# The first expert layer in scaled fp16 hi/lo pairs instead of f32r pairs, with whole-matrix staging

## The chip, the core and the metric

One core of one Trainium2 chip runs the whole program. The metric is the device time of one execution in microseconds (us); lower is better. TensorE (PE) does the matrix products, and loads the stationary operand of each (PEld). VectorE (DVE), ScalarE (ACT) and GpSimd (POOL) do the elementwise work. SyncE (SP) issues most of the transfers. Each engine runs its own instructions in their order and waits on semaphores of the others.

## The reference

Attention with a learned position bias comes first, then a dense mixture of four experts, then a routed one of eight.

```python
scores = q @ k.T / 8 + bias(i, j)            # batch 2, 8 heads, 576 tokens, 64 wide
x = softmax(scores) @ v                       # -> x: 1152 tokens x 512
p = domain_probs / (domain_probs.sum(-1) + 1e-9)
out = 0
for e in range(4):                            # _moe_ref, "the first expert layer"
    h = maximum(x @ w1[e], 0)                 # w1[e]: 512 x 1024
    out += p[:, e] * (h @ w2[e])              # w2[e]: 1024 x 512
# _moe2_ref: each token goes to the one of 8 experts (argmax of x @ w_gate),
# out = gate * sigmoid(x @ w_output_gate)[e] * (relu(x @ w1[e]) @ w2[e])
```

All inputs and the output are fp32, and the products must be close to fp32 ones. So each operand is held as a rounded part (hi) and a remainder (lo), and one product is three matmuls: hi·hi, hi·lo and lo·hi.

## The kernel before

The program has three stages. **Attention** works through 72 heads: index n runs from -2 to 77, u = n // 8 is a block of 128 query rows and h = n % 8 the head. One pass of the loop works on several heads at once: `soft_max(n+2)` on DVE, `soft_exp(n+1)` on ACT, `e_trans(n)` on PE, `qk(n+3)` on PE, `split_lo(n-1)` on DVE and `av(n-2)` on PE. `qk` needs `qt`, the transposed queries of four heads, whose halves two DMAs swap between partitions (L154, L155). The position bias of a block pair goes from `bo` by DMA into the tile `bias` (L311). The last block (u = 8) holds the ends of both batches, so its bias tile (`bias4`) takes two such DMAs for each piece; they are issued in passes n = 45 to 51. The attention weights `eth`/`etl` and v are already fp16 pairs.

**The first expert layer** is one loop over 96 passes i = 8·m + f, where m = 3·e + c is an expert and a chunk of 384 tokens and f a block of 128 hidden columns. Pass i does `l1(i)`, 12 matmuls of 384 columns, and `l2(i-2)`, 9 matmuls of 512 columns; the last eight blocks of l2 run as `l2_tile`. Between them ACT writes the hi part and DVE the lo part of h.

**The second expert layer** runs 13 slots of 128 gathered tokens. While its slot 0 runs, DVE and PE make a table of slots (`slot_table`, three steps), and SP reads its result to choose the expert whose weights it loads.

Every operand of the first expert layer is an f32r pair, 4 bytes an element. A weight matrix is four pieces of 512 KB. Each piece is loaded into a small staging tile (`st`, two of them, L438), and split into two big tiles by ACT and DVE (L457, L458) or, for six pieces that fall into the attention stage (the table `W0`), by POOL alone (L454, L455). The next load is issued when a piece is split. The order of instructions on each engine is the order of the code; the compiler moves a few matmuls of the first l1 ahead of the last attention work. The eight big tiles (`bigt`) are handed out as earlier ones are released. The attention's v is divided by a power of two found on chip (`vP`, its reciprocal `vR`), and `av_norm` (L405) multiplies that back.

Of the kernel before, what the change touches and what calls it, by code (L numbers as in the profile page):

```python
# [24 lines left out]
FF = 1024  # L25
# [25 lines left out]
W0 = {54: (1, 0), 57: (1, 1), 64: (1, 2), 66: (1, 3), 69: (2, 0), 71: (2, 1)}  # L51
# [4 lines left out]
def attn_moe_moe_kernel(ctx, tc, q, k, v, w1, b1, w2, dp, mw1, mw2, wg, wog, ew1, ew2, cst, lmc, out):  # L56
# [5 lines left out]
    st_p = ctx.enter_context(tc.tile_pool(name="st", bufs=2))  # L62
    attn = ExitStack()
# [335 lines left out]
    def av_norm(g):  # L399
        u = g // 2  # L400
        po = av_t.pop(g)
        if g % 2 == 0:
# [10 lines left out]
    xth = xtl = None  # L413
# [21 lines left out]
    def stage():
        e, w, k = pieces[len(staged)]
        t = st_p.tile([128, FF], F32, tag="st", name="st")
        sp.dma_start(out=t.rearrange("p (a d) -> p a d", a=2) if w == 2 else t, in_=msrc[w][e, k])  # L438
        staged[e, w, k] = t

    def pair(e, w, kinds):
        ts = [bigt(f"w{w}{e}", F32R, None) if p is big else p.tile([128, 4 * FF], F32R, tag="wx", name=f"w{w}{e}") for p in kinds]
        wt[e, w] = [[t[:, k * FF:k * FF + FF] for k in range(4)] for t in ts]

    def half(e, w):
        t = bigt(f"w{w}{e}", F32R, None)
        for i, l in enumerate(wt.setdefault((e, w), [[], []])):
            l += [t[:, k * FF:k * FF + FF] for k in (2 * i, 2 * i + 1)]

    def wsplit(e, w, k, on_pool=False):  # L450
        hi, lo = (l[k] for l in wt[e, w])
        t = staged[e, w, k]
        if on_pool:
            pool.tensor_tensor(out=hi, in0=t, in1=one.to_broadcast([128, FF]), op=ALU.mult)  # L454
            pool.tensor_tensor(out=lo, in0=t, in1=hi.bitcast(F32), op=ALU.subtract)  # L455
        else:
            act.copy(hi, t)  # L457
            dve.tensor_tensor(out=lo, in0=t, in1=hi.bitcast(F32), op=ALU.subtract)  # L458
        staged[e, w, k] = None
        if len(staged) < len(pieces):  # L460
            stage()

    with tc.manual_schedule():
# [76 lines left out]
        for n in range(-2, NT + 6):  # L540
# [698 lines left out]
```

## Time and profile before

| what | value |
|---|---|
| median of 3 runs | 855.02 us (850.95 to 857.32) |
| the profiled execution | 852.49 us |
| its span, first to last instruction | 850.6 us |
| busy PE / PEld / DVE / ACT / POOL | 793.2 / 671.2 / 490.7 / 392.8 / 181.6 us |
| mean granted TensorE clock | 0.987 |
| attention | 0 to about 251.7 us of the span |
| first expert layer | about 251.7 to 670 us |
| second expert layer | about 670 us to the end |

Busy time says which engine works, not which one sets the end: matmuls overlap in the records, and a matmul's time is best read from the distance between two starts. The granted clock is 1.00 at 2.4 GHz and 0.50 at 1.2 GHz. What ends an idle stretch stands in brackets behind a row of the timeline. The profiled execution lies 2.5 us below the median and 1.9 us above its own span; the sums below are made against its 852.49 us.

### The profile page before, as it was taken

The page shows a single profiled execution, that of the slowest core. Times are in us where ns is not written, and L with a number is a line of the kernel's source. Part 1 is how long each engine was busy: PE and PEld are TensorE (multiplying, and loading weights), DVE is VectorE, ACT ScalarE, POOL GpSimd, SP SyncE. Part 2 cuts the span into 40 slices and gives each one's busy share as a digit, 9 for nine tenths or more (in the row PEclk, how much of TensorE's full clock was granted, in tenths as well). Part 3 has the DMA queues.
Part 4 walks back from the last instruction along what each step waited for, and adds up shares of the span by engine and source line. Part 5 has one row for each costly group of instructions (what it writes and reads, how often), then busy time and mean ns, then how long its engine had stood idle before and what let it go on. Part 6 is the DMA issues. An engine that isn't in the chain of part 4 may idle for free.

```text
span 850.6 us, 14183 instructions
## 1 busy us (share of the span) xinstructions
PE 793.2 (93%) x5449; PEld 671.2 (79%) x5449; DVE 490.7 (58%) x880; ACT 392.8 (46%) x639; POOL 181.6 (21%) x157
## 2 busy tenths in 40 slices
PE   1877999997989999999999999999999879999996
PEld 0345778776879999999999999999997668888885
DVE  4989999995773312342214322142146859989993
ACT  1657899995643111231113211121123448888883
POOL 6737556651740000000000000000002022211110
PEclk9999999999999999999999999999999989999998
DMA  9944445579423100140002300010037639857720
GB/s 210 167 60 81 94 96 105 105 116 154 126 75 99 51 5 1 47 128 25 1 0 86 113 1 1 1 49 1 1 118 250 212 102 392 292 217 245 254 75 18
DMA packets 56984, 88.75 MB, mean 104 GB/s; under 512 B 18188, under 2 KB 26636, under 8 KB 56910
## 3 DMA queue, kind: packets, MB, share of 16 engines
q1 hardware_dynamic: 53152, 81.61, 36.0%
q0 software_dynamic: 2160, 6.06, 2.1%
q8 instruction: 45, 0.74, 0.4%
q10 hardware_dynamic: 1598, 0.11, 0.1%
q14 instruction: 29, 0.24, 0.1%
HBM read 82.75 MB, written 5.79 MB: 104 GB/s over the span
## 4 chain that ended last, share of the span: by engine, by line
PE 62%; issue 5%; DVE 3%; DMA 3%; ACT 1%; POOL 0%; POOLq 0%; DVEq 0%; ACTq 0%
PE hps L672 8%; PE hps L673 8%; PE hps L674 8%; PE yps L694 7%; PE yps L693 7%; PE yps L692 7%; PE l L994 5%; PE l L1023 5%; DMA out_x<-o,gs 2%; PE sc L324 1%; PE hp L1010 1%; DVE e L950 1%; PE lgp L779 1%; DMA raw<-in_moe_w 1%; PE etp L350 1%
## 5 line engine op out<-in xcount | busy, mean ns | idle before, releaser
L680 DVE SCALAR_TENSOR_TENSOR h<-hps,h 128x384 fp32r<-128x384 f32 x94 | 52.4, 557 | 256.5 <-ACT h L679 256.4
L679 ACT ACTIVATE h<-hps 128x384 fp32r<-128x384 f32 x94 | 46.2, 491 | 298.3 <-PE hps L674 298.3
L672 PE MATMUL hps<-xth,w 128*128 128x384 f32 x384 | 130.1, 339 | 0.0
L673 PE MATMUL hps<-xtl,w 128*128 128x384 f32 x384 | 129.6, 337 | 0.0
L674 PE MATMUL hps<-xth,w 128*128 128x384 f32 x384 | 129.2, 337 | 0.0
L950 DVE TENSOR_TENSOR e<-raw,e 128x1024 fp32r<-128x1024 f32 x104 | 121.1, 1220 | 7.8 <-ACT e L949 6.2
L694 PE MATMUL yps<-w,h 128*128 128x512 f32 x264 | 104.3, 395 | 0.0
L693 PE MATMUL yps<-w,h 128*128 128x512 f32 x264 | 104.0, 394 | 0.0
L692 PE MATMUL yps<-w,h 128*128 128x512 f32 x264 | 103.8, 393 | 0.0
L949 ACT CAST e<-raw 128x1024 fp32r<-128x1024 f32 x104 | 102.0, 1065 | 0.0
L966 POOL DMA_INDIRECT xg<-ydr,ids_e x3 | 5.1, 1691 | 396.0 <-DMA ydr<-y 395.4
L285 DVE TENSOR_SCALAR r<-lm,s,nb 128x576 f32<-128x576 f32 x89 | 75.6, 896 | 0.0
L673 PEld LDWEIGHTS hps<-xtl,w 128*128 128x128 f32 x384 | 72.2, 188 | 3.7
L672 PEld LDWEIGHTS hps<-xth,w 128*128 128x128 f32 x384 | 72.1, 188 | 3.7
L324 PE MATMUL sc<-kt,qt 128*128 128x288 f32 x320 | 61.8, 318 | 12.3 <-DVE mn L333 6.3
L674 PEld LDWEIGHTS hps<-xth,w 128*128 128x128 f32 x384 | 72.1, 188 | 0.0
L333 DVE CUSTOM_DVE_ANT_0 ns<-sc,bias 128x576 f32<-128x576 f32 x72 | 54.3, 754 | 23.0 <-PE sc L324 12.6
L324 PEld LDWEIGHTS sc<-kt,qt 128*128 128x128 f32 x320 | 45.9, 192 | 17.6 <-DVE mn L333 11.0
L694 PEld LDWEIGHTS yps<-w,h 128*128 128x128 f32 x264 | 49.6, 188 | 11.5
L343 ACT ACTIVATE e<-ns,mn 128x576 f32<-128x576 f32 x72 | 56.4, 783 | 0.0
L693 PEld LDWEIGHTS yps<-w,h 128*128 128x128 f32 x264 | 49.6, 188 | 8.0
L692 PEld LDWEIGHTS yps<-w,h 128*128 128x128 f32 x264 | 49.6, 188 | 7.6
(245 smaller groups left out, 1468.6 us busy)
## 6 DMA issues: line engine op xcount, KB each, us to landing
raw<-in_moe_w SPq DMA_DIRECT2D x104, 512.0 KB
st<-in_moe_w SPq DMA_DIRECT2D x32, 512.0 KB
bias<-bo SPq DMA_DIRECT2D x40, 288.0 KB
qt<-qt SPq DMA_DIRECT2D x40, 128.0 KB
ydr<-y SPq DMA_DIRECT2D x8, 258.0 KB
q<-in_q SPq DMA_DIRECT2D x8, 256.0 KB
kraw<-in_k SPq DMA_DIRECT2D x4, 512.0 KB
vraw<-in_v SPq DMA_DIRECT2D x8, 256.0 KB
```

What stands on the lines that cost most here:

```text
L285: (dve if on == "v" else pool).tensor_scalar(out=r, in0=src, scalar1=sc, scalar2=nb1, op0=ALU.mult, op1=ALU.max)
L324: pe.matmul(pt[:, z, 0:288], lhsT=t[w][:, h % 4, :], rhs=kk[:, h, z * 288:z * 288 + 288], start=(i == 0), stop=(i == len(seq) - 1))
L333: dve.tensor_tensor_reduce(out=ns.rearrange("p (z j) -> p z j", z=2), in0=pt[:, :, 0:288], in1=bias_t[u // 2][:, h, :].rearrange("p (z j) ...
L343: act.activation(out=e_t[n // 2][:, (h % 2) * S:(h % 2) * S + S], in_=ns, func=AF.Exp, scale=-1.0, bias=mn)
L672: pe.matmul(ps, lhsT=wh[k][:, fs], rhs=xth[:, c, k, :], start=(k == 0), stop=False)
L673: pe.matmul(ps, lhsT=wh[k][:, fs], rhs=xtl[:, c, k, :], start=False, stop=False)
L674: pe.matmul(ps, lhsT=wl[k][:, fs], rhs=xth[:, c, k, :], start=False, stop=(k == 3))
L692: pe.matmul(acc[m][t], lhsT=hh, rhs=wh[f // 2][:, ws], start=(f == 0), stop=False)
L693: pe.matmul(acc[m][t], lhsT=hh, rhs=wl[f // 2][:, ws], start=False, stop=False)
L694: pe.matmul(acc[m][t], lhsT=hl, rhs=wh[f // 2][:, ws], start=False, stop=(f == 7))
L949: act.copy(hi[:, k, :], raw[w][:, k, :])
L950: dve.tensor_tensor(out=lo[:, k, :], in0=raw[w][:, k, :], in1=hi[:, k, :].bitcast(F32), op=ALU.subtract)
```

## The change

It holds x, h and the weights of the first expert layer as fp16 pairs. fp16 has a small range of exponents, so each operand is scaled. x is multiplied by 8 in `av_norm`, and keeps v's power of two, which is put into the gate weights `pr` later. For each weight matrix the largest magnitude is found: four DVE reductions (`w_max`), one more over these, then a bounce through DRAM (`w_scale`: 128 maxima are written out, and read back into every partition as a row of 128), and a short DVE chain that makes the power of two P and the factor R. The scales go back out through `pr`, with the constant `YS`. The weights are loaded as a whole matrix into one big tile (`w_load`), since a matrix can't be split before its scale is known, and are split into one fp16 tile that holds hi and lo. ACT now writes every hi part with the scale; the lo part is one DVE instruction, or two on POOL for the four pieces of the first matrix. The table `plan` says in which pass a matrix is loaded, reduced and split. The second step of `slot_table` moves from the end of slot 0's first layer to behind the first six matmuls of slot 1's. [...]

```diff
-W0 = {54: (1, 0), 57: (1, 1), 64: (1, 2), 66: (1, 3), 69: (2, 0), 71: (2, 1)}
+W0 = {59: 0, 62: 1, 65: 2, 68: 3}
+XS = 8.0
+WS = {1: 2.0, 2: 16384.0}
+YS = 1.0 / (XS * WS[1] * WS[2])
...
+    def w_load(e, w):
+        t = wraw[e, w] = bigt("wraw", F32, None)[:, :4 * FF].rearrange("p (k f) -> p k f", k=4)
+        for k in range(4):
+            sp.dma_start(out=t[:, k].rearrange("p (a d) -> p a d", a=2) if w == 2 else t[:, k], in_=msrc[w][e, k])
+    def w_max(e, w, k):
+        dve.tensor_reduce(out=wm[:, k:k + 1], in_=wraw[e, w][:, k], axis=AX.X, op=ALU.max, apply_absolute_value=True)
+    def w_scale(e, w, q):
+        c = 2 * e + w - 1
+        dve.tensor_reduce(out=wm[:, 4:5], in_=wm[:, 0:4], axis=AX.X, op=ALU.max)
+        scr = ws_p.tile([128, 1], F32, name=f"scr{c}")
+        q.dma_start(out=scr, in_=wm[:, 4:5])
+        q.dma_start(out=wmb, in_=bass.AP(scr.tensor, scr.offset, [[0, 128], [1, 128]]))
+        yield
+        P, R = wP[:, c:c + 1], wR[:, c:c + 1]
+        dve.tensor_reduce(out=P, in_=wmb, axis=AX.X, op=ALU.max)
...
+    def w_split(e, w, k, on_pool=False):
+        hi, lo = wt[e, w][:, k, 0], wt[e, w][:, k, 1]
+        t, R = wraw[e, w][:, k], wR[:, 2 * e + w - 1:2 * e + w]
+        act.activation(out=hi, in_=t, func=AF.Copy, scale=R)
         if on_pool:
...
+            dve.scalar_tensor_tensor(out=lo, in0=t, scalar=R, in1=hi, op0=ALU.mult, op1=ALU.subtract)
...
+            if n == 44:
+                w_load(0, 1)
+            if 53 <= n < 57:
+                w_max(0, 1, n - 53)
+            if n == 57:
+                ws = w_scale(0, 1, pool)
+                next(ws)
+                w_tile(0, 1)
+            if n == 58:
+                next(ws)
             if n in W0:
-                wsplit(0, *W0[n], on_pool=True)
+                w_split(0, 1, W0[n], on_pool=True)
+            if n == 64:
+                w_load(0, 2)
+            if 70 <= n < 74:
+                w_max(0, 2, n - 70)
+            if n == 74:
+                ws = w_scale(0, 2, pool)
+                next(ws)
...
-            pe.matmul(ps, lhsT=wh[k][:, fs], rhs=xth[:, c, k, :], start=(k == 0), stop=False)
+            pe.matmul(ps, lhsT=w[:, k, 0, fs], rhs=xt[:, c, 0, k, :], start=(k == 0), stop=False)
...
+        plan = {(0, 2): (None, None, 0), (1, 1): (0, 4, 12), (1, 2): (5, 14, 20), (2, 1): (17, 26, 32), (2, 2): (25, 37, 43),
+                (3, 1): (37, 49, 56), (3, 2): (48, 60, 67)}
...
-        side = [[last, steps[2], steps[2], steps[2]], [(0, 0), last, lambda: x_in(1)], [(0, 1), tabs, last, last, (0, 2)], [(0, 3), tabs]]
+        side = [[last, steps[2], steps[2], steps[2]], [(0, 0), last, lambda: x_in(1)], [(0, 1), tabs, last, last, (0, 2)], [(0, 3)]]
...
-        side = [[], [lambda: h_in(0)], [last, lambda: ids_in(3)], [tabs]]
+        side = [[tabs], [lambda: h_in(0)], [last, lambda: ids_in(3)], [tabs]]
```

**SP's order in attention passes 42 to 47.** Before, the last DMA of `bias3` is followed by those of `bias4`, and then by the two qt swaps of pass 46 (a number behind a name tells tiles apart; the brackets hold what the instruction waits for, DMAHW being the lane that the transfer takes):

```order
L155 DMA qt_2569<-qt_2569 64x512 [waits DMAHW7_49]
L311 DMA bias3_1928<-bo_2604 16x8x576 [waits DMAHW0_49,Activation_49]
L311 DMA bias4_2695<-bo_2696 16x8x576 [waits DMAHW1_49,DVE_49,Activation_49]
L311 DMA bias4_2695<-bo_2696 16x8x576 [waits DMAHW2_49]
L154 DMA qt_2764<-qt_2764 64x512 [waits DMAHW3_49,Activation_49]
L155 DMA qt_2764<-qt_2764 64x512 [waits DMAHW4_49]
```

The same stretch now:

```order
L163 DMA qt_2574<-qt_2574 64x512 [waits DMAHW7_49]
L319 DMA bias3_1933<-bo_2609 16x8x576 [waits DMAHW0_49,Activation_49]
L446 DMA wraw_2700<-in_moe_w1 128x1024 [waits DMAHW1_49,DVE_49]
L446 DMA wraw_2700<-in_moe_w1 128x1024 [waits DMAHW2_49]
L446 DMA wraw_2700<-in_moe_w1 128x1024 [waits DMAHW3_49]
L446 DMA wraw_2700<-in_moe_w1 128x1024 [waits DMAHW4_49]
L319 DMA bias4_2705<-bo_2706 16x8x576 [waits DMAHW5_49,DVE_49,Activation_49]
L319 DMA bias4_2705<-bo_2706 16x8x576 [waits DMAHW6_49]
L162 DMA qt_2774<-qt_2774 64x512 [waits DMAHW7_49,Activation_49]
L163 DMA qt_2774<-qt_2774 64x512 [waits DMAHW0_49]
```

Four loads of 512 KB each now stand ahead of the bias transfers and of the qt swaps on the same queue.

**DVE's order in attention passes 57 to 59.** Before, from the end of pass 57:

```order
L362 SCALAR_TENSOR_TENSOR etl_3252<-etp_3206,eth_3215 128x512 [waits Activation_49]
L333 ISA ns_3302,mn_3303<-sc_3270,bias3_1928 128x576 [waits PE_49,Activation_49]
L333 ISA mn_3303 128x1
L405 TENSOR_SCALAR rc_3305<-avp_3154,vR_108 128x4 [waits PE_49]
L408 RECIPROCAL rc_3305<-rc_3305 128x4 [waits DVE_49]
L410 TENSOR_TENSOR x_3139<-avp_3154,rc_3305 128x256 [waits DVE_49]
L362 SCALAR_TENSOR_TENSOR etl_3312<-etp_3238,eth_3250 128x512 [waits Activation_49]
L333 ISA ns_3343,mn_3344<-sc_3314,bias3_1928 128x576 [waits PE_49,Activation_49]
```

Now, from the reduction that starts the bounce of the first matrix:

```order
L453 TENSOR_REDUCE wm_112<-wm_112 128x1 [waits DVE_49]
L341 ISA ns_3308,mn_3309<-sc_3275,bias3_1933 128x576 [waits PE_49,Activation_49]
L341 ISA mn_3309 128x1
L413 TENSOR_SCALAR rc_3311<-avp_3161 128x4 [waits PE_49]
L416 RECIPROCAL rc_3311<-rc_3311 128x4 [waits DVE_49]
L418 TENSOR_TENSOR x_3146<-avp_3161,rc_3311 128x256 [waits DVE_49]
L370 SCALAR_TENSOR_TENSOR etl_3318<-etp_3243,eth_3255 128x512 [waits Activation_49]
L459 TENSOR_REDUCE wP_110<-wmb_113 128x1 [waits DMASW1_49]
L460 TENSOR_SCALAR wP_110<-wP_110 128x1 [waits DVE_49]
L461 TENSOR_SCALAR wP_110<-wP_110 128x1 [waits DVE_49]
L462 RECIPROCAL wR_111<-wP_110 128x1 [waits DVE_49]
L341 ISA ns_3354,mn_3355<-sc_3320,bias3_1933 128x576 [waits PE_49,Activation_49]
```

(A fifth small instruction of the chain, L463, stands ahead of the last row.) One pass of work lies between the reduction L453 and L459, which waits for both DMAs of the bounce on POOL's queue and is ahead of the next `soft_max` (L341).

**DVE's order where the first expert layer begins.** Before, behind the last `av_norm` and the last x:

```order
L405 TENSOR_SCALAR rc_3990<-avp_3857,vR_108 128x4 [waits PE_49]
L408 RECIPROCAL rc_3990<-rc_3990 128x4 [waits DVE_49]
L410 TENSOR_TENSOR x_3847<-avp_3857,rc_3990 128x256 [waits DVE_49]
L429 TENSOR_TENSOR xtl_1079<-xtp_3994,xth_1078 128x4x128 [waits Activation_49]
L680 SCALAR_TENSOR_TENSOR h_4075<-hps_4062,h_4075 128x384 [waits Activation_49,Pool_49]
L458 TENSOR_TENSOR w20_4059<-st_3840,w20_4059 128x1024 [waits DMAHW3_49,Activation_49]
```

The same place now:

```order
L413 TENSOR_SCALAR rc_4008<-avp_3871 128x4 [waits PE_49]
L711 SCALAR_TENSOR_TENSOR h_4094<-hps_4081,h_4094 128x384 [waits Activation_49,Pool_49]
L416 RECIPROCAL rc_4008<-rc_4008 128x4 [waits DVE_49]
L418 TENSOR_TENSOR x_3861<-avp_3871,rc_4008 128x256 [waits DVE_49]
L453 TENSOR_REDUCE wm_112<-wm_112 128x1 [waits DMASW0_49]
L437 TENSOR_TENSOR xt_1084<-xtp_4016,xt_1084 128x4x128 [waits Activation_49]
L459 TENSOR_REDUCE wP_110<-wmb_113 128x1 [waits DMASW3_49]
L460 TENSOR_SCALAR wP_110<-wP_110 128x1 [waits DVE_49]
L462 RECIPROCAL wR_111<-wP_110 128x1 [waits DVE_49]
L465 TENSOR_SCALAR pr_107<-pr_107,wP_110 128x9 [waits DVE_49]
L479 SCALAR_TENSOR_TENSOR w20_4103<-wraw_3594,wR_111,w20_4103 128x1024 [waits Activation_49]
```

(Two small rows of the chain, L461 and L463, are left out here.) The bounce of the second matrix starts behind the last x, and the first split of that matrix (L479), which the first block of l2 needs, stands behind it.

## Rows read from the trace of the kernel before

**Rows 1.** Stretches: length, busy time of PE, PEld, DVE, ACT, POOL, clock, DMA, GB/s.

```profile
263.00:640.00 377.00, 377.00 (x1938) 342.07 (x1937) 107.83 (x198) 70.04 (x121) 0.00 (x0) 1.00 0.13 40
```

**Rows 2.** PE's waits from 262 us to the end: total, times, longest.

```profile
PE pi L917 <- DVE nl L914: 6.2, 1, 6.2
```

**Rows 3.** PE's timeline in the first expert layer: start us, length us.

```profile
302.07 0.33 PE L672 MATMUL hps<-xth,w 128*128 128x384 f32 x1
...
304.18 0.39 PE L692 MATMUL yps<-w,h 128*128 128x512 f32 x1
...
306.27 0.33 PE L672 MATMUL hps<-xth,w 128*128 128x384 f32 x1
```

**Rows 4.** PE's timeline in attention: fp16 matmuls of `av` and `av_end`.

```profile
187.36 0.21 PE L383 MATMUL avp<-v,eth 128*128 128x65 f16 x1
...
187.74 0.72 PE L350 MATMUL etp<-cs,e 128*128 128x128 f32 x4
...
193.94 0.22 PE L395 MATMUL avp<-vz,tlh 128*128 128x130 f16 x1
...
194.29 0.70 PE L350 MATMUL etp<-cs,e 128*128 128x128 f32 x4
```

**Rows 5.** Groups of weight loads: count, busy us, mean ns, idle before.

```profile
L673 PEld LDWEIGHTS hps<-xtl,w 128*128 128x128 f32 x384 | 72.2, 188 | 3.7
...
L385 PEld LDWEIGHTS <-etl 128*128 128x128 f16 x256 | 24.2, 100 | 0.0
```

**Rows 6.** SP's timeline in attention: start of issue, length.

```profile
176.54 6.24 SPq L311 DMA_DIRECT2D bias<-bo  x3
184.98 0.50 SPq L154 DMA_DIRECT2D qt<-qt  x1
...
196.19 0.51 SPq L154 DMA_DIRECT2D qt<-qt  x1
```

**Rows 7.** PE's timeline in attention: the two waits for qt, in brackets.

```profile
193.09 0.64 PE L324 MATMUL sc<-kt,qt 128*128 128x288 f32 x3 [1.42 <-DMA qt<-qt]
...
206.07 0.64 PE L324 MATMUL sc<-kt,qt 128*128 128x288 f32 x3 [3.26 <-DMA qt<-qt]
```

**Rows 8.** Stretches around the second wait, columns as in rows 1.

```profile
202.00:204.00 2.00, 0.82 (x8) 0.61 (x6) 0.89 (x3) 1.75 (x3) 1.10 (x2) 1.00 1.11 109
...
208.00:210.00 2.00, 2.00 (x19) 1.78 (x19) 1.63 (x6) 1.26 (x2) 0.00 (x0) 0.50 1.00 335
```

**Rows 9.** Groups of DVE instructions, columns as in rows 5.

```profile
L333 DVE CUSTOM_DVE_ANT_0 ns<-sc,bias 128x576 f32<-128x576 f32 x72 | 54.3, 754 | 23.0 <-PE sc L324 12.6 <-ACT xth L425 4.6 <-DMA bias<-bo 2.7
L362 DVE SCALAR_TENSOR_TENSOR etl<-etp,eth 128x512 f16<-128x512 f32 x72 | 49.1, 683 | 0.0
L228 DVE TENSOR_REDUCE vmx<-vraw 128x1 f32<-128x2304 f32 x2 | 5.1, 2540 | 0.0
```

**Rows 10.** POOL's timeline: a DMA through POOL's queue, and what waited for it.

```profile
693.69 0.60 POOL L839 DMA_DIRECT2D ydr<-y  x1 [36.42 <-DVE vl L935]
697.17 1.50 POOL L966 DMA_INDIRECT xg<-ydr,ids_l  x1 [2.87 <-DMA ydr<-y]
```

**Rows 11.** Timeline of attention's end.

```profile
245.23 1.90 POOL L454 TENSOR_TENSOR w<-st,one 128x1024 fp32r<-128x1024 f32 x1
...
245.38 1.79 DVE L641 TENSOR_SCALAR prs<-prs 128x9 f32<-128x9 f32 x1
...
247.45 2.15 DVE L643 TENSOR_TENSOR pr<-pr,prs 128x36 f32<-128x36 f32 x1
...
250.26 0.22 PE L385 MATMUL avp<-v,etl 128*64 128x65 f16 x1 [2.83 <-DVE etl L362]
```

**Rows 12.** Timeline of the first expert layer's first l2.

```profile
258.08 0.39 PE L692 MATMUL yps<-w,h 128*128 128x512 f32 x1
```

**Rows 13.** Timeline around the slot table.

```profile
685.18 0.39 PE L917 MATMUL pi<-nl,msel 128*128 128x16 f16 x9 [6.22 <-DVE nl L914]
685.42 4.64 PE L994 MATMUL l<-e,xs 128*128 128x512 f32 x12
```

More of the change, by code (lines that the diff above doesn't have):

```diff
@@ L424, in x_hi @@
         c = u % 3 * 128
-        act.copy(xth[:, u // 3, :, c:c + 128], xp_t[u])
+        act.copy(xt[:, u // 3, 0, :, c:c + 128], xp_t[u])
     def x_lo(u):
         c = u % 3 * 128
-        dve.tensor_tensor(out=xtl[:, u // 3, :, c:c + 128], in0=xp_t.pop(u),
-                          in1=xth[:, u // 3, :, c:c + 128].bitcast(F32), op=ALU.subtract)
-    wt, pieces, staged = {}, [(e, w, k) for e in range(4) for w in (1, 2) for k in range(4)], {}
+        dve.tensor_tensor(out=xt[:, u // 3, 1, :, c:c + 128], in0=xp_t.pop(u),
+                          in1=xt[:, u // 3, 0, :, c:c + 128], op=ALU.subtract)
@@ L433, in attn_moe_moe_kernel @@
+    wt, wraw = {}, {}
     msrc = [None, mw1.rearrange("e (k p) f -> e k p f", p=128), mw2.rearrange("e (k a p) d -> e k p a d", p=128, a=2)]
[L435 to L443, printed above, removed]
@@ L459, in wsplit @@
-        staged[e, w, k] = None
-        if len(staged) < len(pieces):
-            stage()
+            pool.tensor_tensor(out=t, in0=t, in1=R.to_broadcast([128, FF]), op=ALU.mult)
+            pool.tensor_tensor(out=lo, in0=t, in1=hi, op=ALU.subtract)
+        else:
+            dve.scalar_tensor_tensor(out=lo, in0=t, scalar=R, in1=hi, op0=ALU.mult, op1=ALU.subtract)
     with tc.manual_schedule():
@@ L684, in l2 @@
         e, c = divmod(m, 3)
-        wh, wl = wt[e, 2]
+        w = wt[e, 2]
         if f == 0:
@@ L1053, in attn_moe_moe_kernel, with w_step @@
     with tc.manual_schedule():
-        half(0, 2)
-        pair(1, 1, [big, wx_p])
-        when = {}
-        for e, w, s0 in ((0, 2, -2), (1, 1, 4), (1, 2, 24), (2, 1, 28), (2, 2, 48), (3, 1, 52), (3, 2, 72)):
-            for k in range(4):
-                if s0 + k >= 0:
-                    when[s0 + k] = (e, w, k)
-        kinds = {(1, 2): [big, big], (2, 1): [big, big], (2, 2): [big, wx_p], (3, 1): [big, big], (3, 2): [big, big]}
+        plan = {(0, 2): (None, None, 0), (1, 1): (0, 4, 12), (1, 2): (5, 14, 20), (2, 1): (17, 26, 32), (2, 2): (25, 37, 43),
+                (3, 1): (37, 49, 56), (3, 2): (48, 60, 67)}
+        todo = {}
+        scales = {(0, 2): ws}
+        for x, (ld, mx, sp_) in plan.items():
+            if ld is not None:
+                todo.setdefault(ld, []).append(("load", x))
+                for k in range(4):
+                    todo.setdefault(mx + k, []).append(("max", x, k))
+                todo.setdefault(mx + 4, []).append(("bounce", x))
+            for k in range(4):
+                todo.setdefault(sp_ + k, []).append(("split", x, k))
+        def w_step(i):
+            for what, x, *k in todo.get(i, ()):
+                if what == "load":
+                    w_load(*x)
+                elif what == "max":
+                    w_max(*x, *k)
+                elif what == "bounce":
+                    scales[x] = w_scale(*x, sp)
+                    next(scales[x])
+                else:
+                    if k[0] == 0:
+                        next(scales[x])
+                        w_tile(*x)
+                    w_split(*x, *k)
         rts = {83: route([0, 1, 2]), 91: route([3, 4, 5])}
@@ L1067, in attn_moe_moe_kernel @@
                 l2(*divmod(i - 2, 8))
-            if i in when:
-                if when[i][2] == 0 and when[i][:2] in kinds:
-                    pair(*when[i][:2], kinds[when[i][:2]])
-                wsplit(*when[i])
+            w_step(i)
             if i == 12:
```

85 lines of the change are left out of this document (42 added, 43 removed).

## The prediction

> **What bounds the kernel now.** I read three views in this order: the stretches (which engine is busy in which stage), PE's waits, and PE's timeline for the distance between starts. In 377 us of the first expert layer PE is busy for all 377.00 us at clock 1.00 (2.4 GHz), while DVE works 107.8 and ACT 70.0 us [rows 1]. From there to the end PE's longest wait is 6.2 us at the slot table [rows 2]. So in this stage the end is set by how fast PE issues matmuls, and by nothing else. The timeline gives that pace: 12 matmuls of 384 columns from 302.07 to 304.18 are 175.8 ns each, 9 of 512 columns from 304.18 to 306.27 are 232.2 ns each [rows 3]. At 2.4 GHz their columns alone are 160.0 and 213.3 ns. So 15.8 and 18.9 ns of each are not columns.
>
> Attention is different. PE there waits for others: twice for the swapped queries, 1.42 us up to 193.09 and 3.26 us up to 206.07 [rows 7]. The first swap was issued at 184.98 and the second at 196.19 [rows 6], so each took 8 to 10 us, behind bias transfers that move at 109 GB/s [rows 8]. This queue matters for the change.
>
> **Part 1: fp16 matmuls, all on the path.** No matmul is added or removed: 96 x 12 = 1152 of 384 columns and 96 x 9 = 864 of 512. Attention shows fp16 pairs: 12 matmuls of 64 or 65 columns in 0.38 us, 31.7 ns each where the columns are 26.9; 6 of 130 columns in 0.35 us, 58.3 ns each where the columns are 54.2 [rows 4]. The extra is 4.8 ns and 4.1 ns, the same at twice the width, so I take 4.5 ns as a fixed extra: 164.5 and 217.8 ns. That saves 11.3 x 1152 = 13.0 us and 14.4 x 864 = 12.4 us, together 25.4 us. The weight loads don't stand in the way: an fp16 load takes 100 ns where an f32r one takes 188 [rows 5], and at 31.7 ns a pair the loads are already overlapped. The bounds: if instead the cost is per column, 58.3 / 130 = 0.449 ns, the times are 172.3 and 229.7 ns and the saving is 4.0 + 2.2 = 6.2 us; if nothing but columns is left it is 18.2 + 16.3 = 34.5 us. I choose the fixed extra since two widths agree on it.
>
> The Trainium skill, page "TensorE: Matmul & The Clock Gate", section "Back-to-back issue gap", gives N / 2.4 plus 2.5 ns for a warm matmul, which is near these rows. By it the saving would be 13.3 x 1152 + 16.4 x 864 = 29.5 us, an estimate from that page. The same section also has a figure that speaks against the change; it is a rival below.
>
> **Part 2: the first matrix's load moves from pass 52 to pass 44.** Before, SP issued two pieces after all the bias transfers of block 8. Now four pieces, 2.1 MB, stand ahead of them and of the swaps. SP has nothing to wait for there, so they follow the first of three bias DMAs issued from 176.54 [rows 6]. At 335 GB/s, the rate of the stretch in which such pieces moved [rows 8], they occupy the queue for 6.3 us, until about 186; the first `bias4` pair was issued by 182.8 (176.54 + 6.24). So everything behind is some 4 us later, and PE's first wait of 1.42 us grows by 4 (bounds 0 and 6.3). The second wait moves with it and stays. Before, the clock fell to 0.50 after the second wait [rows 8]; a wait of 5 us will likely do the same: 1 us more (0 to 2).
>
> **Part 3: maxima and the first bounce, on DVE in attention.** No row shows a reduction of 1024, but one of 2304 takes 2.54 us [rows 9], so 1.13 each. The four of passes 53 to 56 partly fall into PE's second wait; ACT's four hi parts lie beside. I take 1.5 us (0 to 4.5). The bounce is two DMAs through POOL's queue, one behind the other. One such DMA took from 693.69 to 697.17, 3.5 us, until the next instruction went on [rows 10]; two are 7.0 us. DVE has one pass of work meanwhile, 0.75 + 0.68 us [rows 9] and some 0.9 us of small ones, 2.3 in all, and then stands still ahead of the next `soft_max`. Behind it hang `qk`'s PSUM, `soft_exp` and all of the pass. 4.7 us of standing still, less what slack there is: 4 us (0 to 7).
>
> The Trainium skill, page "DMA: Bandwidth & Descriptors", section "Anatomy of one DMA — SWDGE (gpsimd) path", puts the fixed cost of one such DMA at about 2.0 us. By it the two would take 4 us and this term would be 1 to 2 us, the one in part 5 some 3 us less. The row is dearer than the page, and I stay with the row.
>
> **Part 4: attention's end.** Two tiny DVE instructions took 1.79 and 2.15 us while POOL's split ran beside them, and PE waited 2.83 us for what followed [rows 11]. POOL no longer splits there. Eight small instructions at about 0.2 us and one reduction of 1.13 take the place of that 4.2 us: -1.5 us (-3 to 0). The other three reductions lie beside PE's last `av`.
>
> **Part 5: the second bounce, at the start of the expert layer.** The first l2 started at 258.08 [rows 12], after three l1 blocks. Now it needs a split that needs the scale. The bounce starts behind the last x on DVE, about 254.5; plus 7.0 us [rows 10], a chain of six small instructions (1.2 us) and ACT's hi part (1 us) gives 263.7, less the 1.5 us of part 4. PE is there at about 257. So it stands still for 5.5 us (0 to 8), and the clock is likely to fall again as it did before: 1 us (0 to 2).
>
> **Part 6: the rest.** Of the 6.2 us wait for the slot table [rows 13], six matmuls are now done first. Afterwards twelve ran in 4.64 us, so six are 2.3 us: -2 us (-2.3 to 0). The other six matrices' reductions, chains and splits cost nothing: DVE has 269 us idle in 377 [rows 1], against about 27 us of reductions added; the bounces have two passes (8 us) or more. If that cover were gone, l2 of a new expert would wait.
>
> **Sum.** -25.4 + 4 + 1 + 1.5 + 4 - 1.5 + 5.5 + 1 - 2 = -11.9 us against the profiled execution's 852.49, so 840.6. The median of the runs is 2.5 us above that execution, so I put it at 842.
>
> **The rivals.**
> A. *fp16 costs per column what it costs at 130 columns.* Then the change doesn't do what it is made for: 852.5 - 6.2 + 13.5 = 859.8, with the step to the median about 861, slower than before. It decides where the saving falls under 13.5 us, that is where l1's distance stays above about 170 ns. For it: 0.449 ns a column also fits the 65-column rows within 3 ns, and l1's f32r pace is only 2% above it. Against it: those rows fit a fixed extra better. Chance 0.11.
> B. *Staging takes it all back.* The queue and the two bounces stop attention at three places; with the upper bounds of parts 2, 3 and 5 for most of them the costs are about 24 us: 852.5 - 25.4 + 24 = 851, no change. For it: attention already waits on this queue. Against it: parts of these waits fall into one another. Chance 0.18.
> C. *Attention absorbs nearly all.* The bounces return faster than row and the loads fill idle queue time: costs about 2 us, 829. Chance 0.12.
> D. *The fp16 weight loads are not wholly hidden under long matmuls.* Priced with an extra of 28 ns, above the largest extra of any row here (18.9 ns), the distances are 188 and 241 ns: 14 + 8 us lost instead of gained, 852.5 + 22 + 13.5 = 888. Against it stand the 31.7 ns pairs. Chance 0.03. The Trainium skill, page "TensorE: Matmul & The Clock Gate", section "Back-to-back issue gap", gives this: about 81 ns for a stream of load and matmul pairs at 128 columns, some 28 ns above their columns; the trace does not agree, with 58.3 ns at 130.
>
> **How the numbers follow.** The forecast holds 0.56, with its own range 832 to 850. The range for all reaches from 829 (C's time) to 861 (A's time), which leaves out about half of C, half of A, and D. About 1% (8.5 us) is what a measurement of this kernel can tell from no change. Under 846.5: 0.50 of the forecast and 0.12 of C. Over 863.6: about 0.05 of A, and D. The rest is within 1%.
>
> **What will show it.** The distance of l1's starts at 164 and l2's at 218 ns; at 172 and 230 rival A holds. PE's wait for qt near 193 at about 5 us. A wait of DVE for POOL's DMA of 4 to 5 us in attention, and PE's first l2 waiting some 5 us. The stretch 263 to 640 of before should be 23 us shorter. I am wrong if the distance hardly moves, if an l2 waits for a late split in the middle of the layer, or if attention's end moves by over 15 us.

## The result, and the profile after

The changed kernel takes 859.2 us (median of 16 runs) where the kernel before takes 854.5: a ratio of 1.0052 (95% interval 1.0032 to 1.0071). The forecast was 842, faster; it is slower by half a per cent. The profiled execution is 858.74 us with a span of 856.9 us and a mean granted clock of 0.964 (0.987 before).

PE's timeline in the first expert layer shows the pace that part 1 is about:

```profile
320.72 0.33 PE L706 MATMUL hps<-xt,w 128*128 128x384 f16 x1
...
322.67 0.38 PE L723 MATMUL yps<-w,h 128*128 128x512 f16 x1
...
324.61 0.33 PE L706 MATMUL hps<-xt,w 128*128 128x384 f16 x1
```

Twelve matmuls of 384 columns start 162.5 ns apart and nine of 512 columns 215.6 ns apart, against 175.8 and 232.2 [rows 3]. The fp16 stream gains what was forecast and a little more. So the loss is elsewhere. PE's waits over the whole program (total, times, longest) name the places:

```profile
PE yps L723 <- ACT w L474: 12.6, 1, 12.6
PE xtp L429 <- DVE mn L341: 8.6, 1, 8.6
...
PE pi L948 <- DVE nl L945: 5.6, 1, 5.6
...
PE sc L332 <- DMA qt<-qt: 3.9, 2, 3.6
...
PE hps L706 <- DVE h L711: 2.4, 3, 1.1
```

The first two are new. Two instructions named there as releasers had only just waited themselves; the timeline of DVE, POOL and PE around them shows for whom:

```profile
219.15 0.15 DVE L453 TENSOR_REDUCE wm<-wm 128x1 f32<-128x4 f32 x1
...
219.61 0.79 POOL L455 DMA_DIRECT2D scr<-wm  x1 [3.44 <-DVE wm L453]
227.48 0.59 POOL L456 DMA_DIRECT2D wmb<-scr  x1 [7.08 <-DMA qt<-qt]
...
231.06 0.28 DVE L459 TENSOR_REDUCE wP<-wmb 128x1 f32<-128x128 f32 x1 [7.69 <-DMA wmb<-scr]
...
232.90 1.11 PE L429 MATMUL xtp<-cs,x 128*128 128x128 f32 x4 [8.56 <-DVE mn L341]
...
269.23 0.15 DVE L453 TENSOR_REDUCE wm<-wm 128x1 f32<-128x4 f32 x1
...
277.15 0.56 POOL L456 DMA_DIRECT2D wmb<-scr  x1 [6.47 <-DMA scr<-wm]
...
281.48 0.29 DVE L459 TENSOR_REDUCE wP<-wmb 128x1 f32<-128x128 f32 x1 [10.28 <-DMA wmb<-scr]
...
283.76 0.59 PE L723 MATMUL yps<-w,h 128*128 128x512 f16 x1 [12.61 <-ACT w L474]
```

Each bounce takes 12 us from the reduction L453 to the instruction that reads its result: 219.15 to 231.06, 269.23 to 281.48 (in the runs below up to 13.9 us). POOL's first wait in it is put down to qt, but ends when the write of `scr` has landed, as the second does. The view of DMA issues gives the two halves (KB each, us from issue to landing):

```profile
scr<-wm POOLq DMA_DIRECT2D x2, 0.5 KB, 7.3
...
wmb<-scr POOLq DMA_DIRECT2D x2, 64.0 KB, 3.9
```

Behind the second bounce PE also runs slowly. Stretches of 2 us (columns as in rows 1), and the long stretch of rows 1:

```profile
274.00:276.00 2.00, 0.00 (x0) 0.00 (x0) 0.00 (x0) 0.00 (x0) 0.00 (x0) 0.50 0.00 0
...
288.00:290.00 2.00, 2.00 (x7) 0.91 (x6) 0.35 (x1) 0.00 (x0) 0.00 (x0) 0.50 0.00 0
...
292.00:294.00 2.00, 2.00 (x12) 0.98 (x11) 1.27 (x2) 1.25 (x2) 0.00 (x0) 1.00 0.00 0
...
263.00:640.00 377.00, 361.29 (x2012) 193.31 (x2011) 153.61 (x274) 77.76 (x128) 2.53 (x10) 0.98 0.10 33
```

PE stopped at about 271.2, the granted clock fell to 0.50 at about 273.7 and came back to 1.00 at about 290.7, after 7 us of work at half pace. In those 7 us nine l2 and seven l1 matmuls ran 0.43 and 0.32 us apart: 9 x 0.21 + 7 x 0.16 = 3.0 us lost. The stretch that was PE's alone before [rows 1] now holds 16 us without PE. Behind the first bounce the clock fell as well: it is 0.50 from about 229.3 to 236.1, and PE works again from 232.90.

The starts of the same instruction in both traces give the account, in us (before, after, later by, of which new since the line above):

| instruction | before | after | later | new |
|---|---|---|---|---|
| last bias product | 196.66 | 202.43 | +5.8 | +5.8 |
| last score product | 240.68 | 255.83 | +15.2 | +9.4 |
| last transposition of x | 253.24 | 269.57 | +16.3 | +1.2 |
| first l2 | 258.08 | 283.76 | +25.7 | +9.4 |
| last l1 | 645.26 | 650.13 | +4.9 | -20.8 |
| last product of the expert layer | 669.87 | 675.65 | +5.8 | +0.9 |
| last product of all | 842.56 | 848.35 | +5.8 | 0.0 |

### The profile page after: what moved, and what is told of

It reads as the page before. It is cut to its first block, busy times and chain, and to the rows that moved or that the text cites. A ratio compares the mean times of both kernels' runs of the same rounds, so it can differ in the third digit from the quotient of the medians.

```text
span 856.9 us, 14254 instructions
## 1 busy us (share of the span) xinstructions
PE 776.8 (91%) x5449; PEld 512.0 (60%) x5449; DVE 533.2 (62%) x970; ACT 401.0 (47%) x645; POOL 175.7 (21%) x157
## 4 chain that ended last, share of the span: by engine, by line
PE 66%; DMA 12%; DVE 9%; issue 8%; ACT 2%; POOL 1%; SPq 1%; POOLq 0%; DVEq 0%; ACTq 0%
PE hps L706 6%; PE hps L708 6%; PE hps L707 6%; PE yps L724 6%; PE yps L725 6%; PE yps L723 6%; PE l L1025 5%; PE l L1054 5%; PE sc L332 4%; PE etp L358 3%; PE bp L308 3%; DMA scr<-wm 2%; DVE r L293 2%; DMA out_x<-o,gs 2%; DMA qt<-qt 2%
## 5 line engine op out<-in xcount | busy, mean ns | idle before, releaser
L710 ACT ACTIVATE h<-hps 128x384 f16<-128x384 f32 x96 | 46.8, 488 | 257.3 <-PE hps L708 251.4
L711 DVE SCALAR_TENSOR_TENSOR h<-hps,h 128x384 f16<-128x384 f32 x96 | 53.3, 556 | 181.5 <-ACT h L710 181.5
L706 PE MATMUL hps<-xt,w 128*128 128x384 f16 x384 | 125.7, 327 | 2.4 <-DVE h L711 2.4
L707 PE MATMUL hps<-xt,w 128*128 128x384 f16 x384 | 125.6, 327 | 0.0
L708 PE MATMUL hps<-xt,w 128*128 128x384 f16 x384 | 125.6, 327 | 0.0
L723 PE MATMUL yps<-w,h 128*128 128x512 f16 x264 | 100.8, 382 | 12.6 <-ACT w L474 12.6
L724 PE MATMUL yps<-w,h 128*128 128x512 f16 x264 | 100.8, 382 | 0.7 <-DVE w L479 0.7
L725 PE MATMUL yps<-w,h 128*128 128x512 f16 x264 | 100.8, 382 | 0.0
L332 PE MATMUL sc<-kt,qt 128*128 128x288 f32 x320 | 64.1, 327 | 11.6 <-DVE mn L341 6.3
L341 DVE CUSTOM_DVE_ANT_0 ns<-sc,bias 128x576 f32<-128x576 f32 x72 | 54.3, 755 | 25.3 <-PE sc L332 14.5
L707 PEld LDWEIGHTS <-w 128*128 128x128 f16 x384 | 37.7, 98 | 31.7 <-issue 3.8
L706 PEld LDWEIGHTS <-w 128*128 128x128 f16 x384 | 37.9, 99 | 29.0 <-issue 0.6
L293 POOL TENSOR_SCALAR r<-lm,s,nb 128x576 f32<-128x576 f32 x20 | 45.8, 2288 | 43.9 <-PE bp L308 43.9
L474 ACT ACTIVATE w<-wraw,wR 128x1024 f16<-128x1024 f32 x32 | 36.5, 1142 | 37.2 <-DVE wR L463 30.3
L358 PE MATMUL etp<-cs,e 128*128 128x128 f32 x288 | 52.8, 307 | 1.3 <-DVE etl L370 1.1
L364 ACT ACTIVATE eth<-etp 128x512 f16<-128x512 f32 x72 | 43.2, 600 | 21.2 <-PE etp L358 21.0
```

The source lines that it names most:

```text
L293: (dve if on == "v" else pool).tensor_scalar(out=r, in0=src, scalar1=sc, scalar2=nb1, op0=ALU.mult, op1=ALU.max)
L332: pe.matmul(pt[:, z, 0:288], lhsT=t[w][:, h % 4, :], rhs=kk[:, h, z * 288:z * 288 + 288], start=(i == 0), stop=(i == len(seq) - 1))
L358: pe.transpose(pt[:, jb, :], e[:, c0 + jb % 2:c0 + 256:2], idn)
L706: pe.matmul(ps, lhsT=w[:, k, 0, fs], rhs=xt[:, c, 0, k, :], start=(k == 0), stop=False)
L707: pe.matmul(ps, lhsT=w[:, k, 0, fs], rhs=xt[:, c, 1, k, :], start=False, stop=False)
L708: pe.matmul(ps, lhsT=w[:, k, 1, fs], rhs=xt[:, c, 0, k, :], start=False, stop=(k == 3))
```

## The two bounces

The first theory: three separate stalls (the load on SP's queue, bounce 1, bounce 2) eat the gain and add up. In three runs the DMAs of one or both bounces are left out:

```diff
+        own = (e, w) in ((0, 1), (0, 2))
+        if not own:
...
+            q.dma_start(out=scr, in_=wm[:, 4:5])
+            q.dma_start(out=wmb, in_=bass.AP(scr.tensor, scr.offset, [[0, 128], [1, 128]]))
...
-        dve.tensor_reduce(out=P, in_=wmb, axis=AX.X, op=ALU.max)
-        dve.tensor_scalar(out=P, in0=P, scalar1=1e-30, scalar2=None, op0=ALU.max)
+        dve.tensor_reduce(out=P, in_=wm if own else wmb, axis=AX.X, op=ALU.max)
+        if own:
+            dve.tensor_scalar(out=P, in0=P, scalar1=0.0, scalar2=0.0625, op0=ALU.mult, op1=ALU.add)
```

(This is the edit of the run without both; the runs without one name one matrix. What they leave out is the sharing of the maximum. The constant in its place is right for these inputs alone.)

> The first matrix's scale comes without the two DMAs: the DVE chain reads the maxima of its own partition and puts the constant 0.0625 (which is the power of two of these inputs) in place of the shared maximum; every other instruction stays. Theory (the loss is three separate stalls: the load on SP's queue, the first bounce, the second bounce): PE's wait of 8.6 us at the first bounce goes, with the half clock that follows it (about 1 us), so 859 - 9.5 = about 849.5 (848 to 851). Rival (POOL's slow split of the first matrix is next late, so the gap mostly moves): 855 or more.

Measured: 852.2 us, ratio to the kernel before 0.994 (0.991 to 0.997). Against 1.0052 that is 1.1%, 9.6 us less, as the theory says. (The kernel before took 857.8 us beside this run, so the ratios are compared and not the times.)

> The same for the second matrix alone. Theory: the first l2 starts at about 272 instead of 283.8 us, since only the hi and lo split of one piece is left behind the last maximum, and the clock no longer falls to 0.50 for 17 us at the start of the expert layer (8 of these with PE busy, so 4 us lost): 859 - 11.5 - 4 = about 844 (842 to 847). Rival (the loads and the reductions of the second matrix are late as well, so first l2 waits for these): 851 or more.

Measured: 845.2 us, 0.990 (0.982 to 0.997): 13 us less. The first l2 starts at 272.26, and the clock holds there. A stretch of this run, columns as in rows 1:

```profile
274.00:276.00 2.00, 2.00 (x12) 1.02 (x11) 2.00 (x3) 1.04 (x2) 0.00 (x0) 1.00 0.00 0
```

> Both bounces taken away. Theory (they add up): 859 - 9.5 - 15.5 = about 834 (831 to 837). Rival (one stall covers part of the other, since with attention 9 us shorter the second matrix's load is what comes late): 841 or more.

Measured: 834.8 us, 0.976 (0.970 to 0.982): 2.9%, 25 us less. The savings of the single runs, 9.6 and 13, add up to about this, so neither stall covered the other, and what the rival put next, the second matrix's load, was not late. With no bounce at the start the change gains 2.4% (1.8 to 3.0) on the kernel before.

Does a bounce cost its length, or what no work covers? In the next run both bounces stay, with more passes between issue and use:

```diff
-            if 53 <= n < 57:
-                w_max(0, 1, n - 53)
-            if n == 57:
+            if 49 <= n < 53:
+                w_max(0, 1, n - 49)
+            if n == 53:
                 ws = w_scale(0, 1, pool)
...
-            if 70 <= n < 74:
-                w_max(0, 2, n - 70)
-            if n == 74:
+            if 68 <= n < 72:
+                w_max(0, 2, n - 68)
+            if n == 72:
```

> Both bounces stay, but have more passes to hide in: the first matrix's reductions move from passes 53 to 56 to 49 to 52 and its bounce is issued in pass 53 and read in 58 as now; the second matrix's reductions move to passes 68 to 71 and its bounce is issued in pass 72 instead of 74. Theory (a bounce takes 11 us, and costs what no other work covers): bounce 1 is covered by five passes of about 2.5 us, so 9.5 us go, and some more since DVE was full from 206 to 218; bounce 2 starts 2 to 4 us earlier and the clock still falls: ratio 0.990 (0.986 to 0.994). Rival (the first bounce only moves the late point: POOL's splits or the last reductions are next): ratio 1.000.

Measured: 847.0 us, 0.991 (0.988 to 0.994). DVE's wait for bounce 1 fell from 7.69 to 2.13 us, and for bounce 2 from 10.28 to 7.70; PE's waits behind them from 8.6 to 3.0 and from 12.6 to 9.2. The length stayed (210.17 to 223.06, 257.95 to 270.29), the cost went where work lay beside it.

Next, the reductions as in the last run, and the maxima of the first two matrices shared through TensorE instead of DRAM, a step in a pass (the other six keep their bounces):

```diff
+        pe.transpose(pt[0:1, 2, :], wm[:, 4:5], idn)
+        dve.tensor_reduce(out=vma[:, 0:1], in_=pt[0:1, 2, :], axis=AX.X, op=ALU.max)
+        yield
+        pe.matmul(pt[:, 3, 0:2], lhsT=onr, rhs=vma, start=True, stop=True)
+        yield
...
+        dve.tensor_scalar(out=P, in0=pt[:, 3, 0:1], scalar1=1e-30, scalar2=None, op0=ALU.max)
```

> The scales of the first two matrices are shared through TensorE (a transpose of the 128 maxima, a reduction, and one matmul with ones, a pass each) instead of through DRAM, with the reductions placed as in the run with early maxima; all arithmetic stays. Theory (the 11 us of a bounce are the transfer's fixed time; by TensorE it is under 3 us and in three passes all hidden): PE's two long waits and the half clock at the start of the expert layer go, as in the run without both bounces: ratio 0.974 (0.970 to 0.979). Rival (DVE and PE wait for each other once a pass, and the second matrix's load at about 250 us is late for the earlier reductions): ratio 0.985 or more.

Measured: 836.7 us, 0.979 (0.972 to 0.985), all of the kernel's work done. The timeline of PE and DVE at the second matrix:

```profile
253.86 0.27 PE L473 MATMUL wmp<-cs,wm 128*1 128x128 f32 x1
254.50 0.38 PE L476 MATMUL wmp<-vma,onr 1*128 1x2 f32 x2 [0.37 <-DVE vma L474]
...
258.90 0.38 PE L743 MATMUL yps<-w,h 128*128 128x512 f16 x1 [0.67 <-ACT w L493]
```

From the start of the transposition to the end of the broadcast it takes 1.0 us, and the first l2 waits 0.67 us where it waited 12.6. PE still stands a little for DVE at this place, as the rival says, but its price of 0.985 is only the interval's end.

## Why a bounce takes 12 us

Part 3 priced its two DMAs at 3.5 us each. Seven writes that nothing reads, in the middle of the expert layer, asked which shape is dear:

```diff
+                t = ws_p.tile([p, x], F32, name=nm)
+                pool.dma_start(out=t, in_=xt[0:p, 0].rearrange("p i c t -> p (i c t)").bitcast(F32)[:, 0:x])
```

> Seven writes from on-chip memory to DRAM on POOL's idle queue in the middle of the expert layer, which nothing reads: 128 partitions x 4 bytes (twice), x 64 bytes, x 512 bytes, 1 partition x 512 bytes, 16 partitions x 4 bytes, 1 partition x 4 bytes; issue to landing of each is the result. Theory (many pieces of a few bytes make the write slow): 7 us for 128 x 4 bytes and x 64 bytes, 2 to 3 us for 128 x 512 bytes and 1 x 512 bytes, in between for 16 x 4 bytes. Rival (a small write costs its 7 us whatever its shape, the path to DRAM and back): 7 us for all of them but 128 x 512 bytes.

Measured: 9.6 us for the first 128 x 4 bytes, 9.2, 8.9, 8.5, 8.7 and 8.4 us for the five behind it, 12.0 for the last. This told nothing: POOL had nothing to wait for and issued all seven within 4 us, from 280.5 on, so that each lay behind the first. Apart from each other:

```diff
+            for j, (p, x) in enumerate(probes.get(m, ())):
+                t = ws_p.tile([p, x], F32, name=f"p{m}{j}")
+                pool.dma_start(out=t, in_=y[0:p, 3 * c, 0:x])
```

> Writes to DRAM that nothing reads, on POOL's queue, one at the end of a chunk of the expert layer (31 us apart), their source being rows of y: 128 partitions x 2 KB, 128 x 4 bytes, 128 x 512 bytes, 1 x 2 KB, 1 x 4 bytes, then 128 x 4 bytes twice in a row, then 128 x 2 KB with 128 x 4 bytes behind it; issue to landing is the result. In the run before, seven writes issued together took 8.4 us or more each, whatever their shape. Theory (shape decides once they are apart): 128 x 2 KB in 2.5 to 3.5 us as in the later part of the program, 128 x 4 bytes in 7 us, 1 x 4 bytes in 2 to 3 us. Rival (a write that finds the transfer engines idle takes 7 us whatever its shape; the one that follows another at once is shorter): 7 us for all single ones, 4 us or less for the second of a pair.

Measured, from the view of the probes' tile in one stretch each (128 x 4 bytes, 128 x 512 bytes, 1 x 4 bytes, and the second 128 x 2 KB):

```profile
L738 POOL DMA_DIRECT2D p<-y x1: 547/547/547, 349.9 to 349.9; - x1
DMA to landing us min/median/max: 6.9/6.9/6.9
...
L738 POOL DMA_DIRECT2D p<-y x1: 537/537/537, 381.0 to 381.0; - x1
DMA to landing us min/median/max: 1.8/1.8/1.8
...
L738 POOL DMA_DIRECT2D p<-y x1: 540/540/540, 444.8 to 444.8; - x1
DMA to landing us min/median/max: 1.5/1.5/1.5
...
L738 POOL DMA_DIRECT2D p<-y x1: 539/539/539, 508.5 to 508.5; - x1
DMA to landing us min/median/max: 2.3/2.3/2.3
```

1 x 2 KB took 1.6 us. The 128 x 4 bytes took 6.9, 7.1, 7.4 and 7.3 us, alone, first or second of a pair, and behind a large write. So it is neither the path nor idle engines but the shape: 128 pieces of 4 bytes into one row of 512 bytes take 7 us, one such piece 1.5, the 64 KB of 128 x 512 bytes 1.8. One value stands out: the first 128 x 2 KB took 5.7 us, the second 2.3. The first was issued at 318.70, while the write of a bounce through SP's queue was under way (issued at 313.94, its read at 321.43); the second, at 508.55, with none under way. That a wide write waits behind the 128 small pieces fits this and the run before, but was not tested by itself. Nor was it tested whether the number of small pieces or their lying in one row is what costs. The Trainium skill, page "DMA: Bandwidth & Descriptors", section "Specifications", says that a piece under 512 bytes makes the engine read, modify and write; the single piece of 4 bytes shows no cost of this (1.5 us against 1.6 for 1 x 2 KB), only the 128 in one row could. What happens there inside is not seen.

## The load of the first matrix

The last bias product is 5.8 us late, and PE waits for qt up to 196.38 (3.61 us). The changed kernel's timeline of SP:

```profile
179.09 2.10 SPq L446 DMA_DIRECT2D wraw<-in_moe_w  x4
182.66 1.23 SPq L319 DMA_DIRECT2D bias<-bo  x2
186.09 0.50 SPq L162 DMA_DIRECT2D qt<-qt  x1
```

SP issues the swap 1.1 us later than before (186.09, before 184.98 [rows 6]). The bias product at 170.81 was 1.1 us later too (before 169.69), ahead of the load. So SP does not come to the swap late; the swap takes longer, 10.3 us from its issue to the end of PE's wait, before 8.1.

Is it this place in the queue? The load eight passes earlier:

```diff
-            if n == 44:
+            if n == 36:
                 w_load(0, 1)
```

> The first matrix is loaded in pass 36 instead of 44, ahead of four bias3 transfers instead of those of bias4. Theory (the four pieces hold the queue 6 us at a point where bias transfers and qt swaps have no slack): PE's wait for qt at about 193 falls from 3.6 to under 2 us, the last bias product ends 4 to 6 us earlier, 854 (852 to 856). Rival (the stretch 184 to 212 us is bound by bias transfers whatever stands ahead of them, or the loads hold up qt 20 us earlier instead): 858 to 860.

Measured: 865.8 us, 1.012 (1.005 to 1.018), not faster, and above both ranges; the theory that only this place is dear fell. As the second half of the rival says, the wait went along with the load, and that of before came back behind it: PE is busy 7.72 of 10 us in 170 to 180, where the changed kernel and the one before have 9.97, and 6.79 in 200 to 210, where the kernel before has 6.60. The last bias product still starts 2.3 us earlier (200.12); the bounces behind it took 13.3 and 12.9 us in this execution, which is part of why the time does not show it.

Then through another queue, in the same pass:

```diff
-            sp.dma_start(out=t[:, k].rearrange("p (a d) -> p a d", a=2) if w == 2 else t[:, k], in_=msrc[w][e, k])
+            q.dma_start(out=t[:, k].rearrange("p (a d) -> p a d", a=2) if w == 2 else t[:, k], in_=msrc[w][e, k])
...
-                w_load(0, 1)
+                w_load(0, 1, pool)
```

> The first matrix is still loaded in pass 44, but its four pieces go through POOL's queue instead of SP's; nothing else moves. Theory (order: the bias transfers and the qt swaps stand behind the pieces in one queue): PE's waits for qt fall from 3.9 us together to about the 4.7 us of before at worst, the longest under 2.5 us, and the last bias product ends 3 to 5 us earlier: ratio to the kernel before 1.000 (0.997 to 1.003). Rival (the DMA engines' time: the share is over 1.0 from 184 to 210 us, so the pieces cost their 6 us through any queue): no change against the changed kernel, 1.005.

Measured: 863.1 us, 1.010 (1.004 to 1.017). That is no better than the changed kernel, as the rival says. Its timeline of PE:

```profile
196.67 1.06 PE L332 MATMUL sc<-kt,qt 128*128 128x288 f32 x3 [5.84 <-DMA qt<-qt]
```

The wait is not shorter (with the load in SP's queue it is 3.4 to 6.1 us in the executions here), and the last bias product starts at 201.91. So standing behind the pieces in one queue is not it. What is left is the DMA engines' own time: the four pieces are 2.1 MB, and in 184 to 188 the changed kernel moves 383 GB/s at a share of 1.04. The engines were full there without the pieces: the kernel before has shares of 1.02 and 1.09 in the same two stretches, at 118 and 119 GB/s. Then pieces that are spread should cost less. On the kernel of the TensorE run:

```diff
-            if n == 44:
-                w_load(0, 1)
+            if 31 <= n < 47 and n % 4 == 3:
+                w_load(0, 1, [n // 4 - 7])
```

> The run with the scales through TensorE, with the first matrix's four pieces loaded one at a time in passes 31, 35, 39 and 43 (each right behind a pair of qt swaps) instead of together in pass 44. Theory (four pieces together hold up the qt swaps for 6 us; one holds them up for 1.5 us, which the queue's slack in this part covers): PE's longest wait for qt falls from 3.8 to about 2 us at most, no new one appears, 4 to 5 us less: ratio to the kernel before 0.973 (0.969 to 0.977). Rival (transfers of the last bias blocks set the end of this part by their own time): no change against 0.979.

Measured: 831.8 us, 0.971 (0.965 to 0.976). PE's two waits for qt are 1.10 and 2.08 us, and the last bias product starts at 196.74, 0.1 us after that of the kernel before. The intervals of this run and of the TensorE run overlap, so the 0.8% between them is not clear by the time alone. The last two bias products tell them apart. PE's timelines of the kernel before, the changed kernel and this run have them at:

```profile
189.22 1.18 PE L300 MATMUL bp<-r,w2b 128*32 128x288 f32 x16
...
195.89 1.18 PE L300 MATMUL bp<-r,w2b 128*32 128x288 f32 x16
...
190.33 1.18 PE L308 MATMUL bp<-r,w2b 128*32 128x288 f32 x16
...
201.40 1.44 PE L308 MATMUL bp<-r,w2b 128*32 128x288 f32 x16
...
189.61 1.18 PE L308 MATMUL bp<-r,w2b 128*32 128x288 f32 x16
...
195.97 1.18 PE L308 MATMUL bp<-r,w2b 128*32 128x288 f32 x16
```

The distance is 6.7 us before, 6.4 with spread pieces (in this run and the next), and 9.8 to 12.8 in all ten runs that load them together in pass 44.

## The other six bounces, and the slot table

The prediction priced the bounces inside the layer at nothing, since each has two passes or more. In the changed kernel DVE waits for three of them, 3.97, 5.19 and 5.54 us. These are the three that have two passes (7.8 us at the new pace) before their result is read; of the two with three passes one waits 0.35 us and one not at all. The next run changes the table of the layer, on top of the last one:

```diff
-        plan = {(0, 2): (None, None, 0), (1, 1): (0, 4, 12), (1, 2): (5, 14, 20), (2, 1): (17, 26, 32), (2, 2): (25, 37, 43),
-                (3, 1): (37, 49, 56), (3, 2): (48, 60, 67)}
+        plan = {(0, 2): (None, None, 0), (1, 1): (0, 4, 12), (1, 2): (5, 12, 20), (2, 1): (17, 24, 32), (2, 2): (25, 35, 43),
+                (3, 1): (37, 48, 56), (3, 2): (48, 59, 67)}
```

> The same, and in the table of the expert layer the reductions of five matrices one or two passes earlier, so that each bounce has four passes (15.6 us) before its result is read instead of two or three. Theory (a bounce takes 11 us, so two passes of 3.9 us leave DVE waiting and PE with it for about 2 us at two places): PE's waits for DVE inside the layer go from 4.0 to under 1 us: 0.4 to 0.5% less than the run beside it. Rival (the waits are DVE's own load where splits and reductions meet): no change.

Measured: 825.8 us, 0.962 (0.957 to 0.967): 3.8% under the kernel before, and the fastest here. PE's waits of this run from 250 to 640:

```profile
PE pi L922 <- DVE nr L919: 1.9, 1, 1.9
...
PE hps L728 <- DVE h L733: 0.4, 1, 0.4
```

The waits for h inside the layer went from 2.8 us in the run beside it to 0.4, and DVE no longer waits for a bounce there (16.0 us in the run beside it). That explains 2.4 of the 6 us between the medians, whose intervals overlap at 0.965 to 0.967. In the profiled executions the clock is most of the rest: the run beside it is at 0.50 for 3.4 us from each of about 617, 627 and 648, and this one holds 1.00 from 212 to 659. Half pace for 10.2 us is 5.1 us of work. That the plan brought this about is not shown: PE waits 1.94 and 1.25 us ahead of the last two falls, and about as long at the same two places in this run (1.94 and 1.24), where the clock held.

The last run puts the slot table's second step back:

```diff
-        side = [[tabs], [lambda: h_in(0)], [last, lambda: ids_in(3)], [tabs]]
+        side = [[], [lambda: h_in(0)], [last, lambda: ids_in(3)], [tabs]]
```

(and `tabs` again at the end of the list for slot 0's first layer).

> The changed kernel with the slot table's second step back at the end of slot 0's first layer. Prediction's part 6 (the step moved behind six matmuls is worth 2 us): the stretch from the last matmul of the expert layer to the first of slot 0's second layer goes from 24.4 us to 26.4. Theory from the traces (the table is set by DVE's conversions ahead of it, so PE waits as long either way): 24.4 to 25.2 us, and a ratio of 1.005 to 1.006.

Measured: 859.8 us, 1.004 (1.000 to 1.008), which tells nothing by itself. The stretch is 25.9 us (676.03 to 701.91), between the theory's 25.2 and the prediction's 26.4; it is 24.4 in the changed kernel (675.65 to 700.01) and 24.8 before (669.87 to 694.67). The six matmuls of slot 0 that follow the layer ran at half clock here (2.69 us) and hardly there (1.78), which is 0.9 of the 1.5 us. PE's wait for the table is 6.22 us against 5.56. So the move is worth about 0.6 us. From the table's first matmul (`pn`, here L921) to the one that waits (`pi`, here L948) it takes 8.9 us in this run, in the changed kernel and in the kernel before alike.

## Why the prediction was wrong

- **Part 1 (-25.4) was right in its mechanism and low in size.** 162.5 and 215.6 ns in place of 164.5 and 217.8 give 13.3 x 1152 + 16.6 x 864 = 29.7 us. The fixed extra is 2.4 ns, not 4.5. The Trainium skill's N / 2.4 plus 2.5 ns (page "TensorE: Matmul & The Clock Gate", section "Back-to-back issue gap", where it is the gap of an isolated matmul) agrees with it to 0.3 ns. Rivals A and D fell.
- **Part 2 (+5)** measured 5.8, of which 1.1 us lies ahead of the load. Its reason, the place in SP's queue, was wrong: the same pieces through POOL's queue cost as much, and spread over passes they cost next to nothing. That the DMA engines' time is the reason fits all three runs, and was not measured by itself.
- **Part 3 (+5.5)** measured 9.4, and **part 5 (+6.5)** 9.4 and 3.0 of half clock. This is the step that failed: "One such DMA took from 693.69 to 697.17, 3.5 us", and "two are 7.0 us". The row it was read from was a write of 258 KB in rows of 2 KB [rows 10]; a write of 128 x 4 bytes takes 7 us and the read behind it 4, with issue and hand-over 12 or more. The reductions were priced well: from the last bias product to the last score product it is 44.0 us before, 53.4 here, and 45.7 and 45.2 in the two runs without the first bounce, so at most 1.2 to 1.6 us are left for them (forecast 1.5), and the bounce took 7.7 to 8.2 (forecast 4). Part 5's own times (263.7 less 1.5, and 257) give 5.2 and not 5.5, which changes nothing. Without the two bounces 25 us go, where the prediction had 9.5 us of waits and 1 of clock for them.
- **The clock** was priced at 1 us in parts 2 and 5, and at nothing behind the first bounce, where PE worked 3.2 us at 0.50 (232.9 to 236.1). The wait of 12.6 us was followed by 7 us of work at 0.50. The prediction took the price from falls behind waits of some 3 us [rows 7, 8].
- **Part 4 (-1.5)** measured +1.2: POOL was idle at this place, and the small DVE instructions fell from 4.4 to 1.9 us, but four reductions of 1.21 us lay on DVE ahead of the last `av_norm`.
- **Part 6 (-2)** measured -0.4 in the stretch and about -0.6 by the last run: DVE's own conversions set the table's time, so matmuls put ahead of it shorten PE's wait but not the chain. The row that priced six matmuls at 2.3 us [rows 13] was mostly at half clock; the six moved took 1.55. The bounces inside the layer, priced at nothing, cost PE 1.8 us (two waits for h, 0.70 and 1.05; the third of the 2.4 us lies ahead of the first l2).

By the account: up to the first l2 25.7 us were lost where the parts had 14.1 (parts 2 to 5 without the second 1 us of clock, less 0.4 for three blocks at the new pace); the layer gave back 20.8 where they had 23; and behind it 0.9 us and another 0.5 at the end were lost where they had 3 gained. 11.6 + 2.2 + 4.4 = 18.2 us, the distance between -11.9 and +6.3. Rival B (the staging takes all back, 851) names what happened; its price was still low, since the bounces cost more than the upper bounds it was made from (the second 12.4 us with its clock, bound 8 and 2). That the sign turned is the bounces: the run without them is 2.4% faster than the kernel before.

## What to carry to other kernels

Price a transfer from a row of its own shape, pieces and bytes: a small one can cost more than a large one. A round trip that one engine waits for in its order costs all that lies behind it on that engine, so give it passes of work before it is read, or take a path through PE, which shared 128 maxima in 1.0 us here. A load that was spread over passes cost less here than the same bytes at once, where the DMA engines were full already.

## What was not expected of the hardware

- 128 x 4 bytes into one DRAM row: 6.9 to 9.0 us; 1 x 4 bytes 1.5 us; 128 x 512 bytes 1.8 us.
- After 12.6 us in which PE stood still the granted clock stayed at 0.50 for 7 us of work; in the run without the second bounce, where PE paused for 1.4 us between 270 and 274, it stayed at 1.00.
- The weight loads hardly slow the fp16 stream: 2.4 ns a matmul beyond its columns, where the f32r stream had 15.8 and 18.9 [rows 3].
